# Batch 0's k, v and first expert products in plain f32, and a list scheduler for steps 0 to 17, in a fused attention and mixture-of-experts kernel

## The chip, the cores and the metric

The kernel runs on one core of a Trainium2 chip. Five engines matter here: TensorE (PE in the profile; its weight loads are the row PEld), VectorE (DVE), ScalarE (ACT), GpSimd (POOL), and SyncE (SP), which issues all DMAs of this kernel. Each engine takes its instructions in the order in which the program lists them; engines wait for each other by semaphores.

The metric is the time of one execution in microseconds on the device, as a median of several runs. The profiled execution is one further run, with a time of its own. Its span goes from the first instruction to the last, and the time is a little longer than the span.

## The reference

An attention through 32 memory slots per head, and behind it a mixture of four experts on its output:

```python
# q, k, v: (8, 8, 576, 64)   phi: (8, 8, 576, 32)
a = softmax(phi, axis=2)                                # over the sequence
k_m = einsum('bhsm,bhsd->bhmd', a, k)
v_m = einsum('bhsm,bhsd->bhmd', a, v)
attn = softmax(scale * (q @ k_m.T), axis=-1)            # over the 32 slots
x = (attn @ v_m), heads side by side -> (4608, 512)
p = domain_probs / (domain_probs.sum(-1) + 1e-9)        # (4608, 4)
for e in range(4):                                      # w1: (4, 512, 1024), w2: (4, 1024, 512)
    h = maximum(x @ w1[e], 0)
    out += p[:, e:e+1] * (h @ w2[e])
```

Everything is f32 at the boundary of the kernel.

## The kernel before, in words

**Tiling.** Batches go in four pairs. For each pair and each expert there are 32 steps: two batches, two halves of the rows (256 and 320 rows, or the other way round), eight blocks of 128 of the expert's 1024 hidden columns. That makes 512 steps (LAST). A step s has two parts on TensorE. `first(s)` (L485) makes a block of the hidden layer: six products of 256 or 320 columns. `second(s)` (L489) multiplies it by w2: six products of 512 columns, or nine where an odd batch also closes the tile that the two batches share. `first` runs two steps ahead of `second` (AHEAD), so step s issues `first(s + 2)` and then `second(s)`. Since x = attn · v_m, the kernel never forms x: it multiplies v_m by w1 beforehand (the tile vw), and `first` multiplies the transposed attention (the tile AT) by vw.

**Splits.** Products run in the rounded type fp32r. To keep f32 precision, each operand is split in two: ScalarE copies it rounded (the "hi" part), VectorE or GpSimd subtracts that from the operand (the "lo" part), and a product is made of three: hi·hi, hi·lo, lo·hi (lines L403 to L405, L459 to L461 and L500 to L502). Transposes and scores (L342) are plain f32.

**The beginning.** Before step 0, batch 0 needs: phi's softmax, its transposes (`phi_turn`, L212, and `phi_turn_tail`, L226, into the tile a), splits of k and v (`kv_split`, L249, and `tail_split`, L236), their products with a (`kv_mm`, L259), the folding of the partial sums by transposes (`kv_out`, `kv_fold`, `kv_pick`, L276 to L303) into the tile kvT, scores and softmax (`scores_mm`, L334, `scores_exp`, `soft`), the transposed attention AT (`transposes`, L380), and for one half of the hidden columns (fh = 0) the splits of w1 and the product of v_m with w1 (`vw_mm`, L400, evicted by `vw_out` and `vw_out_by_copy`, L423 and L428). This part is listed by hand from L1292 on. Between its pieces stand matmuls that only keep TensorE busy (`keep_warm`, L1284): 10, 4, 6 and 4 of them.

**Steps 0 to 17** (MANUAL is 18). Beside their own work they carry the remaining work of batch 0 (two more score tiles, the second half of w1 and vw, three quarters of w2) and the whole chain of batch 1, which is needed from step 14 on. REST_0 and UNITS_1 say in which step each whole unit is emitted; within a step the units come first, then `first(s + 2)`, then `second(s)` (L1369). The order on each engine is then made by the compiler's own scheduler. From step 18 on, `schedule()` (L602) has assigned every single operation to a step, and `run_step` (L1237) lists them in a fixed order.

**Loads.** All weights and inputs come through rings of staging buffers (`ring`, L84; `stage_ahead`, L95). A load is issued on SP's queue as soon as the buffer it goes to is free. The first nine loads (`early`) are k and v of batch 0 in four parts, their last 64 rows (kvt), q, two parts of w1 and one of w2. Batch 1 needs the split w1 again: before, the split tiles of the start are kept in SBUF and also written to DRAM (`keep_w1`, L146) for later pairs.

## Time and profile before

| | |
|---|---|
| median of 3 runs | 1372.82 us (1372.54 to 1373.73) |
| the profiled execution's own time | 1374.13 us |
| its span | 1372.4 us |
| granted TensorE clock, mean | 0.999 |
| stores and loads | HBM read 131.41 MB, written 26.21 MB |

The page of the profile gives busy times per engine over the whole span, a chain of work that ended last (followed back from the last instruction), and groups of instructions by line. TensorE's busy time is pipelined, so that consecutive matmuls overlap in the records: the interval between the starts of two matmuls is what one costs, not its duration. The windows view cuts the span into stretches, and the timeline lists the instructions in order with their start, their duration and, in brackets, the idle time of the engine before them and what ended it. Where a row is merged (x8), its duration is that of the whole run of instructions. A plain f32 product stands in the records as two matmuls, an f32 transpose as one.

### The profile page before, as it was taken

What the parts mean: (1) busy time and instruction counts of PE and PEld (TensorE: products, weight loads), DVE (VectorE), ACT (ScalarE), POOL (GpSimd) and SP (SyncE); (2) the same over time, 40 slices, a digit from 0 to 9 for tenths busy, and PEclk for the clock granted to TensorE, in tenths of its full rate; (3) what the DMA queues carried; (4) which work ended last, traced back from release to release, by engine and by line L of the source; (5) the groups of instructions that cost most, each with busy time, mean ns of one, the idle gap of its engine ahead of it and who ended that gap; (6) DMA issues with size and microseconds to landing.
All of it is one profiled execution on the core that took longest, in us unless ns stands there. A gap on an engine that the chain in (4) does not pass through costs nothing.

```text
span 1372.4 us, 21779 instructions
## 1 busy us (share of the span) xinstructions
PE 1356.9 (99%) x7444; PEld 1186.9 (86%) x7444; DVE 834.0 (61%) x1851; ACT 742.7 (54%) x1739; POOL 27.0 (2%) x27
## 2 busy tenths in 40 slices
PE   7999999999999999999999999999999999999998
PEld 6888888888888888888888888888888888888887
DVE  7667667577676656657567565665666644444532
ACT  7545555456556556655555656565655645455321
POOL 4300000000000000000000000000000000000000
PEclk9999999999999999999999999999999999999999
DMA  7627364344666466562664756555465635446101
GB/s 287 227 85 235 98 199 126 111 138 148 170 191 184 141 184 173 159 194 73 185 175 136 219 159 185 146 174 151 146 179 160 174 96 175 128 131 162 31 32 39
DMA packets 102398, 209.41 MB, mean 153 GB/s; under 512 B 18192, under 2 KB 18576, under 8 KB 102288
## 3 DMA queue, kind: packets, MB, share of 16 engines
q1 hardware_dynamic: 102288, 208.03, 50.6%
q8 instruction: 59, 0.97, 0.3%
q14 instruction: 51, 0.42, 0.1%
HBM read 131.41 MB, written 26.21 MB: 115 GB/s over the span
## 4 chain that ended last, share of the span: by engine, by line
PE 95%; DMA 2%; DVE 1%; ACT 1%; SPq 0%; issue 0%; ACTq 0%; DVEq 0%
PE p L501 19%; PE p L502 19%; PE p L500 19%; PE p L459 10%; PE p L461 10%; PE p L460 10%; PE pv L714 3%; PE x L267 2%; PE sT L1030 1%; DMA stage<-w 1%; PE sc L342 1%; PE pv L403 1%; PE pv L405 1%; PE pv L404 1%; DMA stage<-in_kv 0%
## 5 line engine op out<-in xcount | busy, mean ns | idle before, releaser
L481 DVE SCALAR_TENSOR_TENSOR h<-p,h 128x256 fp32r<-128x256 f32 x512 | 215.6, 421 | 319.8 <-ACT h L475 186.9
L501 PE MATMUL p<-w,h 128*128 128x512 f32 x1024 | 404.0, 395 | 0.0
L502 PE MATMUL p<-w,h 128*128 128x512 f32 x1024 | 401.9, 393 | 0.2 <-DVE nm L190 0.2
L500 PE MATMUL p<-w,h 128*128 128x512 f32 x1024 | 401.7, 392 | 0.0
L475 ACT ACTIVATE h<-p 128x256 fp32r<-128x256 f32 x512 | 196.3, 384 | 322.3 <-PE p L461 299.4
L459 PE MATMUL p<-AT,vw 128*128 128x256 f32 (+1 forms) x1024 | 305.7, 299 | 3.0 <-DVE h L481 1.6
L460 PE MATMUL p<-AT,vw 128*128 128x256 f32 (+1 forms) x1024 | 302.2, 295 | 0.6 <-DVE AT L395 0.6
L461 PE MATMUL p<-AT,vw 128*128 128x256 f32 (+1 forms) x1024 | 301.5, 295 | 0.1
L502 PEld LDWEIGHTS p<-w,h 128*128 128x128 f32 x1024 | 192.2, 188 | 43.3 <-DVE nm L190 0.5
L459 PEld LDWEIGHTS p<-AT,vw 128*128 128x128 f32 x1024 | 192.4, 188 | 24.5 <-issue 3.0
L500 PEld LDWEIGHTS p<-w,h 128*128 128x128 f32 x1024 | 192.4, 188 | 23.0
L501 PEld LDWEIGHTS p<-w,h 128*128 128x128 f32 x1024 | 192.6, 188 | 22.7 <-DVE w L155 0.2
L460 PEld LDWEIGHTS p<-AT,vw 128*128 128x128 f32 x1024 | 193.5, 189 | 17.7 <-DVE AT L395 0.8
L461 PEld LDWEIGHTS p<-AT,vw 128*128 128x128 f32 x1024 | 192.6, 188 | 0.3 <-issue 0.3
L722 ACT COPY E<-pv 128x512 f32<-128x512 f32 x192 | 111.4, 592 | 76.8 <-PE pv L714 46.2
L481 DVE SCALAR_TENSOR_TENSOR hm<-p,hm 128x64 fp32r<-128x64 f32 x256 | 56.1, 219 | 155.8 <-ACT h L475 155.7
L475 ACT ACTIVATE hm<-p 128x64 fp32r<-128x64 f32 x256 | 56.9, 222 | 110.8 <-PE p L461 110.6
L710 ACT CAST w<-stage 128x1024 fp32r<-128x1024 f32 x96 | 100.7, 1049 | 4.2 <-DMA stage<-w 4.2
L796 DVE TENSOR_TENSOR w<-stage,w 128x512 fp32r<-128x512 f32 x120 | 79.4, 683 | 0.0
L792 ACT CAST w<-stage 128x512 fp32r<-128x512 f32 x120 | 73.3, 616 | 5.2 <-DMA stage<-in_w 4.9
L776 DVE TENSOR_TENSOR vw<-rows,vw 128x512 fp32r<-128x512 f32 x96 | 64.6, 685 | 10.7 <-ACT vw L772 10.0
L517 DVE SCALAR_TENSOR_TENSOR acc<-p,pt,acc 128x512 f32<-128x512 f32 x96 | 67.3, 742 | 2.7 <-PE p L502 2.6
(135 smaller groups left out, 1321.8 us busy)
## 6 DMA issues: line engine op xcount, KB each, us to landing
stage<-w SPq DMA_DIRECT2D x96, 512.0 KB, 4.2
rows<-E SPq DMA_DIRECT2D x768, 64.0 KB, 2.7
stage<-in_w SPq DMA_DIRECT2D x80, 512.0 KB, 4.4
stage<-in_kv SPq DMA_DIRECT2D x32, 512.0 KB, 4.5
w<-w SPq DMA_DIRECT2D x64, 256.0 KB, 4.7
out<-acc SPq DMA_DIRECT2D x32, 256.0 KB, 4.1
stage<-in_qh SPq DMA_DIRECT2D x24, 288.0 KB, 3.2
ph<-in_phi SPq DMA_DIRECT2D x16, 288.0 KB, 4.1
```

Source lines behind the costliest of these rows:

```text
L459: nc.tensor.matmul(ps, w[:, 0, f], at_t[:, g, 0, c], start=g == 0, stop=False)
L460: nc.tensor.matmul(ps, w[:, 0, f], at_t[:, g, 1, c], start=False, stop=False)
L461: nc.tensor.matmul(ps, w[:, 1, f], at_t[:, g, 0, c], start=False, stop=g == 1)
L475: nc.scalar.activation(t[:, 0, to], ps[:, at_], AF.Relu)
L481: nc.vector.scalar_tensor_tensor(t[:, 1, to], ps[:, at_], 0.0, t[:, 0, to].bitcast(F32), ALU.max, ALU.subtract)
L500: nc.tensor.matmul(po[t], x[:, 0, :], w[:, 0, :], start=j == 0, stop=False)
L501: nc.tensor.matmul(po[t], x[:, 0, :], w[:, 1, :], start=False, stop=False)
L502: nc.tensor.matmul(po[t], x[:, 1, :], w[:, 0, :], start=False, stop=j == NJ - 1)
L710: nc.scalar.copy(w, raws[key])
L722: nc.scalar.copy(box["E"][:, i, :], box[i])
L792: nc.scalar.copy(t[:, 0, :], raws[key][:, i, :])
L796: nc.vector.tensor_sub(t[:, 1, :], raws[key][:, i, :], t[:, 0, :].bitcast(F32))
```

## The change

Three things change, all of them in the beginning and in steps 0 to about 21.

1. **Batch 0's products of a with k and v, and of v_m with the first expert's w1, are made in plain f32** from the staged data. There are no splits of k, v, kvt and w1 for these, and no folding: `direct_mm` puts k (or v) on the stationary side and gets the transposed result at once, which `direct_pick` copies into kvT. `direct_vw` makes vw from two plain f32 products of 512 columns, with both heads of a tile in one product, and evicts it in whole tiles. kvt of batch 0 is loaded in 64 rows instead of 128.
2. **Steps 0 to 17 are ordered by a list scheduler of single operations**, `start_plan`: each copy, subtraction, product, eviction and load is a task with an engine, a duration, predecessors and buffers; a simulated clock picks per engine the task that can start, the most urgent first. The resulting order is the order in the program. Tasks that don't fit before step 18 are emitted in steps 18 to 21. The warm-up matmuls after the first ten are gone.
3. **Who does what, and when it is loaded, changes with it.** Since the first w1 is no longer split, w1 of expert 0 is loaded a second time for batch 1 and split then (four `lo` parts on VectorE, four on GpSimd). Seven of the eight `lo` parts of the first w2 go to GpSimd; those of batch 1's k, v and kvt go from GpSimd to VectorE. The probabilities are loaded before k, and batch 1's phi before w1.

The core of the diff:

```diff
+SPLIT_KV = ("DVE",) * 8
+SPLIT_W2 = ("DVE",) + ("POOL",) * 7
+SPLIT_W1 = ("DVE", "POOL") * NP
...
+LOADS = [("w1", 0, 1, 0), ("w1", 0, 1, 1), ("qm", 0, 1), ("w2", 0, 1), ("w2", 0, 2), ("qt", 0), ("w2", 0, 3)]
+LOADS += [("kvt", 1), ("kv", 1, 0), ("kv", 1, 1), ("kv", 1, 2), ("w1", 0, 0, 0, 1), ("kv", 1, 3)]
+LOADS += [("qm", 1, 0), ("w1", 0, 0, 1, 1), ("qm", 1, 1), ("w1", 0, 1, 0, 1), ("w1", 0, 1, 1, 1), ("qt", 1)]
...
+    def direct_turn_out(g):
+        nc.scalar.copy(st["af"][:, 2 * g:2 * g + 2, :4], st["tpa", 0, g].rearrange("p c a m -> p a c m"))
...
+    def direct_mm(hp, w, raw, tail):
...
+        x, af = st["xd", w, hp // 2][:, hp % 2, :], st["af"]
+        for c in range(4):
+            nc.tensor.matmul(x, raw[:, c, w, :], af[:, hp, c], start=c == 0, stop=False)
+        nc.tensor.matmul(x, tail[:64, hp, w * P:w * P + P], af[:64, hp, 4], start=False, stop=True)
...
+    def direct_vw(fh, g, raw, tag):
+        ps = psum.tile([P, 512], F32, name="pv", tag=tag[0], bufs=tag[1])
+        for i in range(2):
+            nc.tensor.matmul(
+                ps, st["vf"][:, g, P * i:P * i + P], raw[:, i, :], start=i == 0, stop=i == 1
+            )
+        return ps
+
+    def direct_vw_hi(ps, fh, g):
+        vw[0, 0, fh, g] = att.tile([P, 2, 512], F32R, name="vw", tag="vw0", bufs=4)
+        nc.scalar.copy(vw[0, 0, fh, g][:, 0, :], ps)
+
+    def direct_vw_lo(ps, fh, g):
+        t = vw[0, 0, fh, g]
+        nc.vector.tensor_sub(t[:, 1, :], ps, t[:, 0, :].bitcast(F32))
+
+    def direct_pick(g, w, i):
+        kvd, x = kvT[0][:, w, 2 * g:2 * g + 2], st["xd", w, g]
+        r, m = slice(64 * i, 64 * i + 64), slice(M * i, M * i + M)
+        (nc.vector.tensor_copy if i and w == 0 else nc.scalar.copy)(kvd[r, :, m], x[r, :, m])
...
+        while left:
+            best = None
+            for eng in free:
+                cand = None
+                for t in left:
+                    if t.eng != eng or any(d.end is None for d in t.deps):
+                        continue
+                    at0 = max([free[eng]] + [d.end + (0 if d.eng == eng else 200 if d.eng == "PE" else 130) for d in t.deps])
...
+                    if t.sb and eng in lock:
+                        at0 = max(at0, lock["POOL" if eng == "DVE" else "DVE"] - 150)
+                    k = (max(at0, free[eng] + START_LOOK) if at0 > free[eng] + START_LOOK else free[eng], due[t])
+                    if cand is None or k < cand[0]:
+                        cand = k, at0, t
+                if cand and (best is None or cand[1] < best[1]):
+                    best = cand
...
     load_phi(0)
+    nc.sync.dma_start(pt, prob)
     with tc.manual_schedule():
...
-        for s in range(AHEAD):
-            first(s)
-        probabilities()
-    load_phi(1)
-    for s in range(MANUAL):
-        run_plan(s)
-        first(s + AHEAD)
-        second(s)
-    released.update(range(count[1]))
-    stage_released()
+        for t in first_tasks:
+            run_task(t)
```

## The prediction

> **What bounds the kernel now.** I read the page first: the busy shares and the chain that ended last.

> ```profile
> span 1372.4 us, 21779 instructions
> PE 1356.9 (99%) x7444; PEld 1186.9 (86%) x7444; DVE 834.0 (61%) x1851; ACT 742.7 (54%) x1739; POOL 27.0 (2%) x27
> PE 95%; DMA 2%; DVE 1%; ACT 1%; SPq 0%; issue 0%; ACTq 0%; DVEq 0%
> ```

> TensorE is busy 99% of the span and makes 95% of the chain. The change does nothing after step 21 but place a few operations anew, so what it can win is time in which TensorE does less than it could before the end of step 17. I looked for that in the chain of the first 60 us, which also shows what precedes the first hidden block:

> ```profile
> 1.65 6.21 DMA stage<-in_kv
> 7.88 1.15 ACT kvs L255 x2
> 9.05 1.35 DVE kvs L256
> 10.92 0.68 DVE a L224
> ...
> 13.23 1.71 PE x L267 x8
> ...
> 18.16 1.08 PE sc L342 x8
> ...
> 19.72 0.27 ACT kvT L297
> ...
> 20.99 1.12 PE sc L342 x8
> ...
> 25.50 1.27 issue
> ...
> 28.80 0.70 DVE AT L395
> 29.54 0.38 PE p L460
> ...
> 58.79 0.94 PE x L267 x8
> ```

> The first product with k starts near 11 us, although k landed at 7.86 (1.65 + 6.21): splits by ScalarE and VectorE stand between. The scores are complete at 22.1, and `first(0)` goes on only when AT's lo part is written at 29.5. Where step 0 begins and step 17 ends, the timeline of TensorE says:

> ```profile
> 31.25 0.28 PE L459 MATMUL p<-AT,vw 128*128 128x256 f32 x1
> ...
> 35.51 0.28 PE L459 MATMUL p<-AT,vw 128*128 128x256 f32 x1
> ...
> 36.22 0.40 PE L500 MATMUL p<-w,h 128*128 128x512 f32 x1
> ```

> ```profile
> 94.99 0.31 PE L459 MATMUL p<-AT,vw 128*128 128x320 f32 x1
> ...
> 95.87 0.39 PE L500 MATMUL p<-w,h 128*128 128x512 f32 x1
> ...
> 97.26 0.39 PE L500 MATMUL p<-w,hm 128*128 128x512 f32 x1
> ...
> 97.94 0.32 PE L459 MATMUL p<-AT,vw 128*128 128x320 f32 x1
> ```

> 31.25 is the first matmul of `first(2)`, which opens step 0; at 97.94 step 17's `second` has ended. Between lie 66.7 us. A narrow `first` costs 0.71 us (35.51 to 36.22), a wide one 0.88, six products with w2 1.39, nine 2.07. Side work comes from the groups of TensorE from 31.25 to 97.5 us:

> ```profile
> L342 PE MATMUL sc<-kvT,stage 128*128 128x64 f32 (+1 forms) x64 | 7.0, 260 | 0.0
> L403 PE MATMUL pv<-w,vt 128*128 128x512 f32 x12 | 5.2, 432 | 0.0
> L267 PE MATMUL x<-kvs,a 128*128 128x256 f32 x32 | 4.6, 283 | 0.0
> L388 PE MATMUL tp<-ident,at 128*128 128x128 f32 (+1 forms) x14 | 2.1, 268 | 0.0
> L218 PE MATMUL tpa<-ident,ph 128*128 128x128 f32 x8 | 1.4, 275 | 0.6 <-DVE ph L203 0.6
> ```

> By start-to-start intervals the steps' own work is 6 x 0.71 + 12 x 0.88 + 16 x 1.39 + 2 x 2.07 = 41.2 us. The side work is 64 score records at 0.11 (1.73 us for 16 in the row below), 36 vw products (three lines of 12) at 0.23, 32 kv products at 0.118 (58.79: 0.94 for eight), and some 36 short ones (14 + 8 shown, 14 more) at 0.11: 7.0 + 8.3 + 3.8 + 4.0 = 23.1. So 64.3 of 66.7 us are work and **2.4 us are lost** inside the steps. The larger loss lies before 31.25.

> ```profile
> 37.08 0.23 PE p L500
> ...
> 37.77 1.73 PE sc L342 x16
> ```

> **The change, part by part.** Loads and clock come first, from the windows view (columns: length, then busy us and instruction count of PE, PEld, DVE, ACT, POOL, then the granted TensorE clock, DMA share, GB/s).

> ```profile
> 10.00:15.00 5.00, 3.71 (x19) 3.45 (x20) 4.60 (x7) 4.46 (x10) 4.58 (x3) 0.69 1.03 418
> 15.00:20.00 5.00, 4.71 (x40) 4.54 (x40) 3.08 (x8) 2.64 (x10) 1.28 (x2) 0.97 1.03 401
> ...
> 8.50:11.91 3.41, 0.85 (x7) 0.85 (x8) 2.85 (x4) 3.41 (x9) 2.84 (x3) 1.00 1.03 419
> 11.91:15.33 3.42, 3.19 (x15) 2.92 (x15) 3.02 (x4) 2.69 (x6) 3.03 (x2) 0.50 1.03 414
> ...
> 31.25:40.00 8.75, 8.75 (x59) 7.54 (x58) 8.72 (x23) 5.19 (x12) 0.00 (x0) 1.00 0.57 193
> 40.00:50.00 10.00, 8.89 (x48) 7.18 (x47) 8.59 (x21) 7.46 (x16) 5.11 (x4) 1.00 0.79 270
> ...
> 60.00:70.00 10.00, 10.00 (x64) 8.66 (x63) 2.94 (x11) 4.97 (x17) 5.08 (x4) 1.00 0.71 204
> 70.00:97.50 27.50, 27.50 (x162) 23.99 (x161) 19.85 (x48) 11.53 (x30) 0.00 (x0) 1.00 0.29 92
> ```

> *Loads.* DMA moves 401 to 418 GB/s, so 512 KB take 1.28 us. The 72 KB of probabilities now go ahead of k (+0.2), kvt is halved (-0.6), batch 1's phi (576 KB) goes ahead of w1 (+1.4). Landings after that: k/v part 0 at 8.1, kvt 8.7, parts 1 to 3 at 10.0, 11.2, 12.5, q 13.8, phi 15.2, w1 16.5 and 17.7, w2 19.0. SP now waits for the phi transposes (8.4 us) before it issues phi and w1; the queue still holds 5 us of data then, so this costs nothing; without that cover w1 would be late by the wait.

> *Phi.* The transposes end at 8.34 (7.96 + 0.38 below). Three ScalarE copies without subtractions follow (0.58, 0.58, 0.37), on an engine that no longer splits k meanwhile: the last ends at 9.1, and the first direct product starts at 9.3 instead of 11.

> ```profile
> 7.96 0.38 PE L230 MATMUL tpb<-ident,ph 128*128 128x128 f32 x2
> ...
> 8.93 0.58 ACT L223 CAST a<-tpa 128x512 fp32r<-128x512 f32 x1
> ```

> *Direct k and v.* 40 plain f32 products of 64 columns, the form of the scores: two records of 0.108, 0.216 each, 8.7 us. Before it was 36 products in fp32r at 0.118 (4.2 us) and eight folds: more TensorE work, but without a hand to ScalarE and VectorE. It keeps up with the loads: k of part 3 can be multiplied by 13.7, the picks take two copies of 0.27 (the row at 19.72), and scores (1.7 us) end by 15.7 instead of 22.1. From there AT took 7.4 us (22.1 to 29.5), with other subtractions between its links on VectorE; even so it would be there by 23.1. v fills TensorE meanwhile.

> *Direct vw.* Two products per tile, 512 columns in plain f32, which no row shows. Lower bound: two records at the fp32r price, 0.46 for a product. Upper: eight times the 64-column product, 1.73. But a record of 64 columns costs as much (0.108) as a transpose of 128 (0.11), so the time doesn't grow with the columns from 64 on; two records of four times 0.11 are 0.88. I take 0.92, next to that row, and keep 1.73 as an end that this speaks against. Two tiles before `first(0)`: 3.7 us; two later ones: 3.7, in place of 12 fp32r products of 0.23 (2.8), so **+0.9** among the side work. For all eight products the ends are worth -3.7 and +6.5 us, half of it before step 0.

> [...]

> *The start as a sum.* TensorE is nearly dense from 9.3: 8.7 + 1.7 + 3.7 + 0.45 (transposes) = 14.6, to 23.9. Then hi (0.58), lo (0.69) and three hand-overs of 0.2: `first(0)` at 25.8. In that gap a side product of second-half vw (1.84 us, its w1 landing near 21) fits. `first(0)` and `first(1)` take 1.4: **step 0 at 27.2 instead of 31.25**.

> *Steps 0 to 17.* Work 41.2 + 23.1 + 0.9 - 1.8 (already done) = 63.4. VectorE, 8.72 of 8.75 us busy from 31.25 to 40, loses the first w1's lo parts and seven of w2's eight, and takes ten of batch 1's; ahead of step 0 it loses all splits. GpSimd gets eleven subtractions (SPLIT_W2, SPLIT_W1). I take a loss of 3.0 us: 2.4 as now and 0.6 because the order is fixed on assumed durations. Any task moved to steps 18 to 21 is the same work later, and TensorE has no idle cover to lose there; I count it at zero. The second load of w1 (2 MB, 5 us of DMA) and its eight splits fall where DMA runs at 92 to 204 GB/s, and its splits replace those of the first; should they be late, they delay vw of batch 1, and with it step 14.

> The sum: 27.2 + 63.4 + 3.0 = 93.6 against 97.94: **-4.3 us**. Profiled execution: 1374.13 - 4.3 = 1369.8. That execution lies 1.3 above the median, so against 1372.82 the forecast is **1368.5**.

> *The clock.* From 11.91 to 15.33 the granted clock was 0.50, after a window of equal length (8.50 to 11.91) in which TensorE was busy for 0.85 us only. The change takes 14 warm-ups away after that point, but begins at 9.3: about 2.6 of 3.4 us busy in that window. I count full clock. [...]

> **The rivals.**
> - *The new order holds without waits* (1366): loss in steps 1 us or less, second-half work fills the gaps of the start. 27.2 - 0.3 + 63.4 + 1.0 = 91.3, -6.6. For it: VectorE is relieved where it was full. Against: nothing shows that the list's durations hold.
> - *The clock is halved once* (1370.2): TensorE idles too long before 9.3, or the two-record products count for less. One window of 3.41 us at half speed costs 1.7. Against: 2.6 us of work in the window.
> - *The start's gain is given back* (1371.5): every side product stands in a fixed place directly behind its producer. Some 45 such pieces; if each second one comes 0.15 us late, 3 us more are lost (45 / 2 x 0.15 = 3.4). For it: the 0.6 us of idle before L218 in the groups above are exactly such a wait.
> - *VectorE sets the pace: slower* (1377). From 31.25 on to 50 it is 17.3 of 18.75 us busy already, and the list adds ten subtractions of 0.70 for batch 1 (7.0 us) and four of w1 (2.8). If the hidden block's lo part queues behind them, four PSUM buffers fill up and TensorE stops. It decides when more than 7 us of that isn't covered; the seven lo parts of w2 and four of w1 that go in these steps (7.7 us) speak against it.

> That the splits weren't on the path is excluded by the chain (7.88 to 11.6). That loads end later than the products is possible only for w1 (17.7), which leaves 5 us.

> **How the numbers follow.** Forecast 1368.5: 0.50. No waits 1366: 0.15. Clock 1370.2: 0.05. Given back 1371.5: 0.20. Slower 1377: 0.10. A measurement tells apart about 0.2%, 2.7 us: faster means under 1370.1. Faster: 0.50 + 0.15 + about half the clock case = 0.68; same 0.22; slower 0.10. The range goes from 1364.5 (no waits, and f32 products at the lower end before step 0, -1.8) to 1373.0 (given back, and half of the dearer end before step 0, +1.6).

> **What would show it.** Right: first direct product near 9.3; scores done by 16; step 0's first matmul at 26.5 to 28; a direct 512-column product of about 0.92; step 17's end at 92.5 to 94.5; clock 1.00 from 8.5 on. Wrong: TensorE idle in front of side products, for more than 4 us in sum; `first(0)` after 29; VectorE at 100% with TensorE waiting for L481's successor; or a time after step 21 that differs from before by over 1 us.

## The result, and the profile after

The change makes the kernel slower. Six runs gave 1382.01 us (1380.01 to 1382.88) beside 1373.52 us (1372.54 to 1376.94) for six runs of the kernel before; the ratio is 1.0055, with a 95% interval of 1.0042 to 1.0068. The forecast was 1368.5 us. The profiled execution took 1380.01 us with a span of 1378.2 us, 5.8 us longer than before.

The page of the changed kernel, span, busy times and the chain that ended last:

```profile
span 1378.2 us, 21742 instructions
PE 1368.0 (99%) x7444; PEld 1193.0 (87%) x7444; DVE 826.4 (60%) x1834; ACT 733.4 (53%) x1723; POOL 16.3 (1%) x20
...
PE 96%; DMA 2%; DVE 1%; ACT 1%; issue 0%; SPq 0%; ACTq 0%; DVEq 0%
```

The engines that the change relieves are relieved (VectorE 834.0 to 826.4 us, ScalarE 742.7 to 733.4), and TensorE is busy for 11.1 us longer, in the same number of matmul records. So some matmuls take longer, or longer ones stand where shorter ones stood. The chain of the first 60 us shows which:

```profile
3.21 7.88 DMA stage<-in_kv
11.13 1.10 PE xd L278 x8
12.24 0.36 PE xd L279 x2
...
14.25 1.90 PE xd L278 x8
16.15 0.62 PE xd L279 x2
16.76 1.90 PE sc L408 x8
...
30.23 5.55 PE pv L292 x8
35.78 0.44 PE tp L457 x4
```

From 11 us to beyond 50 us the chain is TensorE alone: the splits are gone from it, as forecast. But the same eight records of a direct product of k (L278) take 1.10 us at 11.13 and 1.90 us at 14.25. The granted clock gives the reason, in the windows view cut at the borders where the clock changes (columns as in the prediction: length, busy us and records of PE, ..., granted clock, DMA share, GB/s; the records are all that reach into the window, so those cut by its borders are counted too):

```profile
10.18:13.59 3.41, 2.69 (x21) 2.35 (x20) 0.23 (x1) 0.20 (x1) 0.00 (x0) 1.00 1.02 404
13.59:17.00 3.41, 3.41 (x15) 3.06 (x14) 0.00 (x0) 0.20 (x1) 0.00 (x0) 0.50 1.04 406
...
23.83:27.24 3.41, 3.41 (x15) 3.06 (x15) 1.63 (x5) 1.89 (x6) 0.00 (x0) 0.50 0.38 127
...
30.66:34.07 3.41, 3.41 (x5) 1.35 (x4) 0.00 (x0) 0.82 (x5) 0.00 (x0) 0.50 0.74 269
34.07:37.48 3.41, 3.41 (x13) 1.67 (x12) 1.74 (x3) 1.57 (x3) 0.00 (x0) 1.00 0.94 300
```

The clock halves at 13.59 and stays at 0.50 until 34.07, for 20.48 us. Before, the one stretch at half clock was 3.42 us long (11.91 to 15.33); 20.48 is six times 3.41, and I call that length a window. In all six TensorE is busy 100% of the time. Six windows at half speed are 10.2 us of TensorE's time, and that is about what step 0 is late (its first matmul, and that of `first(20)`, which opens step 18, in the timeline of TensorE):

```profile
40.51 0.68 PE L518 MATMUL p<-AT,vw 128*128 128x256 f32 x1
...
105.96 0.41 PE L518 MATMUL p<-AT,vw 128*128 128x320 f32 x1
```

Step 0 begins at 40.51 instead of 31.25, 9.3 us later, and 13.3 us later than the forecast 27.2. Steps 0 to 17 take 65.5 us instead of 66.7, so that step 18 opens 8.0 us later; 5.8 of these are left at the end of the span, since the two executions also differ by some 2 us behind step 18. The medians lie 8.5 apart.

### The profile page after: what moved, and what is told of

Its sections match the earlier page's. It is cut to its first block, busy times and chain, and to the rows that moved or that the text cites. A ratio compares the mean times of both kernels' runs of the same rounds, so it can differ in the third digit from the quotient of the medians.

```text
span 1378.2 us, 21742 instructions
## 1 busy us (share of the span) xinstructions
PE 1368.0 (99%) x7444; PEld 1193.0 (87%) x7444; DVE 826.4 (60%) x1834; ACT 733.4 (53%) x1723; POOL 16.3 (1%) x20
## 4 chain that ended last, share of the span: by engine, by line
PE 96%; DMA 2%; DVE 1%; ACT 1%; issue 0%; SPq 0%; ACTq 0%; DVEq 0%
PE p L564 19%; PE p L562 19%; PE p L563 19%; PE p L518 10%; PE p L520 10%; PE p L519 10%; PE pv L1174 3%; PE x L339 2%; PE sT L1490 1%; PE xd L278 1%; PE pv L292 1%; DMA stage<-in_kv 1%; DMA stage<-w 1%; PE sc L408 0%; PE pv L481 0%; PE pv L483 0%
```

## The experiments

The theories first. **A**: the clock follows the columns that are streamed through the array in a window, so that products of 64 columns, each record of which comes with a weight load of its own (PE x7444 and PEld x7444 on the page), count for little. **B**: the clock fell because TensorE was idle now and then for a load (2.69 of 3.41 us busy from 10.18 to 13.59), whatever the form of the products. The expectations also name **C**: plain f32 counts for little in any form.

**Loops of one form (e1_forms).** The kernel before, with loops ahead of it whose result is not read:

```diff
+        for _ in range(16):
+            full(512)          # plain f32, 512 moving columns
+        for _ in range(64):
+            full(64)
+        for _ in range(64):
+            full(128)
...
+        for _ in range(120):
+            rounded(256)       # fp32r
```

> The kernel before, with TensorE loops ahead of everything, dense and waiting for nothing: 16 plain f32 products of 512 columns, 64 of 64 columns, 64 of 128 columns, 64 of 64 columns, 120 fp32r products of 256 columns, then 13 times (five plain f32 of 64, one fp32r of 512) and 13 times (five of 64, three of 512). Some 100 to 150 us longer, so only the granted clock by window counts. Theory A (the clock follows the columns that stream through the array in a window, not the time for which TensorE is busy): 1.00 in the 512 block, 0.50 in both 64 blocks from their second window on, 1.00 in the 128 block and the fp32r block, 1.00 in the last. Theory B (the clock fell because of the idle gaps at 10.4 and before 13.6, the form of the products doesn't matter): 1.00 throughout after the first window. Theory C (plain f32 counts for little in any form): 0.50 in the blocks of 512, 64 and 128 columns, 1.00 from the fp32r block on.

Measured: the clock was 1.00 through all blocks, the dense 64-column ones too. That is what B had forecast. It speaks against A as I had put it, and against C and every other reading by which the plain f32 form lowers the clock by itself. A window of the first 64 block:

```profile
25.16:28.57 3.41, 3.41 (x33) 3.41 (x32) 0.00 (x0) 0.00 (x0) 0.00 (x0) 1.00 0.00 0
```

Counted from the timeline by what lies inside the window, with records at its borders by their share, these are some 1960 columns; all counts of columns below are made so. In the changed kernel, the first five windows at half clock hold 840 to 980, because there each record takes 0.2 us and more instead of 0.11. So I changed A to **A2**: one border on the columns per window, at whatever clock. A dense run of 64-column products lies just above it at full clock, and below it at half clock, where it can't get out again.

**Twice the columns (e2_wide).** The direct products of k and v multiply by the matrices a of both head pairs of a tile, and half of the result is not read:

```diff
-            nc.tensor.matmul(x, raw[:, c, w, :], af[:, hp, c], start=c == 0, stop=False)
+            nc.tensor.matmul(x, raw[:, c, w, :], af[:, two, c], start=c == 0, stop=False)
```

> The changed kernel, with 128 moving columns in each direct product of k and v in place of 64 (the matrices a of both head pairs of a tile; half of the result is not read). Same number of products, loads and waits. A: the record of 128 columns costs as much as one of 64 (0.11 us at full clock), the clock stays at 1.00, step 0 begins at 27 to 29 us in place of 40.5, the time falls by 9 to 13 us against the changed kernel, to about 1370 (3 us under the kernel before). B: the clock still halves at about 13.6, comes back one window later; 1374. C: nothing changes, 1380 to 1383.

Measured: 1373.34 us (1371.69 to 1374.75) beside 1374.29 for the kernel before, ratio 0.9987 (0.9978 to 0.9996); 8.7 us under the changed kernel, whose six runs were made in another session. In the profiled execution step 0 begins at 33.7, and the clock fell once and came back after one window. That is the course and the time that B had forecast; A had the clock held and 1370:

```profile
8.33:11.74 3.41, 2.13 (x15) 1.62 (x14) 0.77 (x3) 0.85 (x2) 0.00 (x0) 1.00 1.03 320
11.74:15.16 3.42, 3.42 (x16) 2.97 (x15) 0.23 (x1) 0.21 (x1) 0.00 (x0) 0.50 1.02 399
15.16:18.57 3.41, 3.41 (x26) 2.93 (x25) 0.75 (x2) 0.21 (x1) 0.00 (x0) 1.00 1.03 407
```

At half clock, 16 records of 128 columns bring the clock back, where 15 to 17 records of 64 did not for four windows in a row, at the same busy time. With busy time and records alike, the columns of a record are what differs, so idle time (B) is not what keeps the clock down. For the first fall this run can't tell the two theories apart: the window had 2.13 us busy, and with that only some 1650 columns.

**Filler products (e3_fill1, e4_fill3).** One, or three, bf16 products of 512 columns behind each group of five direct products, their result not read:

```diff
         nc.tensor.matmul(x, tail[:64, hp, w * P:w * P + P], af[:64, hp, 4], start=False, stop=True)
+        for _ in range(1):
+            nc.tensor.matmul(st["fill"], fill, fill.unsqueeze(1).broadcast_to([P, 4, P]), start=True, stop=True)
```

> The changed kernel, with one bf16 product of 512 columns (0.22 us) behind each group of five direct products, eight in all, their result not read. Columns per window rise from about 950 to 2000. A: the clock is held at least from some window on, if the border lies under that; the span is 1369 to 1376. B and C: 0.50 up to about 34 us as before, span 1380.

> The same with three such products behind each group (24 in all, 5.2 us of TensorE time at full clock). A: columns per window of about 3500; clock 1.00 throughout, step 0 begins near 32, span 1373 to 1375. B: halved once at 13.6. C: held as well, because bf16 counts.

Measured, one run each: 1372.2 us (span 1370.4) and 1375.81 us (span 1374.0), the clock at 1.00 throughout in both, as A had it; step 0 at 31.1 and 34.1 (near 32 was expected of the second). Since the fillers also stand in the waits, these two say little against B.

**The border by itself (e5_forms2).** Loops again, now with 32 columns in between:

```diff
+        for _ in range(16):
+            full(512)
+        for _ in range(96):
+            full(32)
+        for _ in range(64):
+            full(64)
+        for _ in range(32):
+            full(128)
+        for _ in range(64):
+            full(64)
```

> The kernel before, with dense TensorE loops ahead of everything: 16 plain f32 products of 512 columns, 96 of 32, 64 of 64, 32 of 128, 64 of 64 columns, none with a gap. Theory A2 (one border on the columns streamed in a window of 3.41 us, at whatever clock; the windows so far put it between 1200 and 1900 recorded columns, and a dense run of 64-column products has 1950 at full clock but 970 at half): 1.00 in the 512 block; the clock halves one window after the 32 block begins (about 960 columns at full clock, TensorE 100% busy); stays 0.50 through the 32 block and the first 64 block; back to 1.00 one to two windows into the 128 block; stays 1.00 in the last 64 block. Theory B (only idle gaps lower the clock): 1.00 throughout.

Measured, in windows of the 512 block, the 32 block (two), the first 64 block, its end with the 128 block, the 128 block, and the last 64 block:

```profile
9.25:12.67 3.42, 3.42 (x9) 1.51 (x9) 1.35 (x1) 0.24 (x1) 1.07 (x1) 1.00 1.03 420
19.49:22.91 3.42, 3.42 (x33) 3.42 (x33) 0.00 (x0) 0.00 (x0) 0.00 (x0) 1.00 0.00 0
22.91:26.32 3.41, 3.41 (x18) 3.41 (x18) 0.00 (x0) 0.00 (x0) 0.00 (x0) 0.50 0.02 5
63.87:67.28 3.41, 3.41 (x18) 3.41 (x18) 0.00 (x0) 0.00 (x0) 0.00 (x0) 0.50 0.00 0
80.93:84.34 3.41, 3.41 (x18) 3.41 (x18) 0.00 (x0) 0.00 (x0) 0.00 (x0) 0.50 0.00 0
84.34:87.76 3.42, 3.42 (x32) 3.42 (x32) 0.00 (x0) 0.00 (x0) 0.00 (x0) 1.00 0.00 0
91.17:94.59 3.42, 3.42 (x33) 3.42 (x32) 0.00 (x0) 0.00 (x0) 0.00 (x0) 1.00 0.00 0
```

All five points of A2 came true. After a window of 33 records of 32 columns, without a gap, the clock halves (22.91). It stays there through the 32 block and the whole first 64 block (63.87: some 1020 columns). It returns with the 128 block (84.34). The last 64 block, which differs from the first only in that it begins at full clock, keeps it (91.17: some 1960 columns). The same products hold two different clocks, 0.50 at 63.87 and 1.00 at 91.17, by the clock at which they begin. B is refuted: TensorE is 100% busy in all seven windows.

The kernel behind the loops shows the same of a window with waits. In e1 and in e5 the first products with k of the kernel before (fp32r, 256 columns) fall differently into the windows; each pair of lines is one such window and the next:

```profile
120.73:124.14 3.41, 1.70 (x13) 1.28 (x12) 2.48 (x4) 3.41 (x8) 2.31 (x2) 1.00 0.50 173
124.14:127.55 3.41, 3.41 (x18) 3.41 (x18) 3.16 (x4) 2.36 (x6) 2.04 (x2) 0.50 0.49 161
```

```profile
108.24:111.65 3.41, 1.91 (x14) 1.73 (x14) 2.53 (x5) 3.41 (x8) 2.75 (x2) 1.00 0.54 173
111.65:115.06 3.41, 2.49 (x22) 2.29 (x21) 3.41 (x4) 1.80 (x5) 1.61 (x1) 1.00 0.55 201
```

1.91 us busy keep the clock in e5, where 2.69 us lost it in the changed kernel. So the first fall can't be put down to idle time either. Columns fit, if a column of fp32r counts about half of one in a plain f32 record: some 2400 of them lost the clock in e1 and some 3400 kept it in e5, beside some 1210 plain f32 columns that lost it in the changed kernel. That half is an estimate from these windows alone. In time, too, a plain f32 record of 512 columns is twice one of fp32r (0.44 against 0.23 us).

**Fillers in the waits alone (e6_gapfill), and with the width (e7_widefill).** Two fillers behind the first k group and one behind the second; once with products of 64 columns, once (e7) on top of the edit of e2, with 128.

```diff
+        for _ in range({(0, 0): 2, (1, 0): 1}.get((hp, w), 0)):
+            nc.tensor.matmul(st["fill"], fill, fill.unsqueeze(1).broadcast_to([P, 4, P]), start=True, stop=True)
```

> The changed kernel with two bf16 products of 512 columns behind the first group of direct products and one behind the second, which lie in the wait for the loads of k, their result not read. A2: columns of the window that fell rise from 1216 to about 2500, the clock mostly stays at 1.00 (the windows' place differs from run to run), step 0 begins at 29 to 31 us in place of 40.5, the step part is unchanged, the time is 2 to 4 us under the kernel before. B: the same for the first fall. If the 64-column groups can't hold the clock even so: 0.50 from 17 to 34 us, time 5 us over the kernel before.

> The same three products, and 128 moving columns in the direct products of k and v. A2: columns well above the border in every window, clock 1.00 in nearly every run; step 0 at 29 to 30.5, time 2.5 to 4.5 us under the kernel before and less spread than without. B: as without the width.

Measured without the width: 1378.22 us, from 1372.05 to 1384.21, in twelve runs, beside 1375.04 (ratio 1.0022, 1.0003 to 1.0041). That is a miss: 2 to 4 us under the kernel before were expected. This spread goes with the clock. The six fastest runs (1372.05 to 1377.47) had a mean granted clock of 0.995 to 0.999, the four slowest (1381.11 to 1384.21) 0.991 to 0.992. One window of half clock in 1380 us is 0.0012 of the mean, so 0.991 is some seven windows. In the profiled execution the fall comes later, in a window without any gap:

```profile
14.72:18.13 3.41, 3.41 (x29) 3.28 (x29) 1.96 (x6) 1.92 (x5) 0.00 (x0) 1.00 1.04 411
18.13:21.54 3.41, 3.41 (x28) 3.14 (x27) 2.58 (x6) 2.06 (x6) 0.00 (x0) 1.00 0.88 288
21.54:24.96 3.42, 3.42 (x8) 1.79 (x7) 2.27 (x2) 1.42 (x6) 1.32 (x1) 0.50 0.85 301
```

Both windows are 100% busy with 64-column records. By what lies inside, some 1770 columns kept the clock and some 1620 lost it. With e2, where some 1650 lost the clock (8.33) and some 1730 at half clock brought it back (11.74), and with a window of e9 that held with some 1680,

```profile
13.78:17.19 3.41, 3.41 (x29) 3.21 (x27) 1.79 (x4) 0.85 (x2) 0.00 (x0) 1.00 1.05 410
17.19:20.60 3.41, 3.41 (x29) 3.19 (x27) 1.53 (x3) 1.89 (x6) 0.00 (x0) 1.00 0.97 309
```

With the width: **1372.60 us (1371.71 to 1373.54), ratio 0.9984 (0.9975 to 0.9993)**, the fastest version of those with more than one run. The clock was 0.999 or 1.000 in all eleven runs, as A2 has it; the fillers are those of e6, so the width is what differs. The gain of 2.4 us is just under what was expected (2.5 to 4.5): step 0 begins at 31.2 and not at 29 to 30.5.

**The half clock of the kernel before (e8_beforewarm).** Ten more warm-up matmuls behind the phi transposes of the kernel before:

```diff
+        keep_warm(10)
```

> The kernel before with ten more warm-up matmuls behind its phi transposes, where TensorE waits from 8.3 to 10.9 us. A2 and B: its one window at half clock (11.9 to 15.3) is gone; what that window cost: at most 1.7 us, and less because splits and loads end last there; 0 to 1.5 us under the kernel before. If it gains nothing, the half clock in the kernel before cost nothing.

Measured: 1374.90 beside 1375.04 us, ratio 1.0001 (0.9992 to 1.0009). The clock was 1.00 in the profile, step 0 began at 30.2 instead of 31.25, and step 18 opened at 98.04, no earlier than before (97.94). So the one halved window cost the kernel before nothing. The kernel before does scatter by its clock, though: over 67 runs beside these experiments it was 0.996 to 1.000, with medians of 1378.5 at 0.996, 1375.5 at 0.997 and 1374.1 to 1374.6 from 0.998 up. Where the further halved windows of those runs lay isn't known.

**Spread fillers, and eight fillers in more runs (e9_spread, e10_fill1b).** Five fillers behind four of the eight groups, the width left at 64 columns; and the kernel of e3 once more, in twelve runs.

```diff
+        for _ in range({(0, 0): 2, (2, 0): 1, (0, 1): 1, (2, 1): 1}.get((hp, w), 0)):
+            nc.tensor.matmul(st["fill"], fill, fill.unsqueeze(1).broadcast_to([P, 4, P]), start=True, stop=True)
```

> The changed kernel with 64 columns again and five bf16 products of 512 columns, their result not read: two in the wait behind the first k group, one each behind the third k group and the first and third v group. A2 (border between 1660 and 1730 recorded columns a window, a dense 64-column window being hardly above it): every window from 8 to 22 us gets at least 500 more; clock 0.998 to 1.000 in at least 9 of 10 runs, where the three products before left it between 0.991 and 0.999. Groups cost 1.29 us against 1.46 with 128 columns: step 0 at 30 to 30.7, 0.5 to 1 us ahead of the wide one, time 2.5 to 4 us under the kernel before. If some runs still fall, they lie 1.7 us up for each halved window.

> The kernel with one such product behind each of the eight groups again, timed in rounds. A2: the clock is held in all runs (2100 or more columns in every window in its profile), step 0 at 31.1, time 1.5 to 3 us under the kernel before: the gain that is left of the change when the clock is held and 1.5 us of fillers are paid. If the change's gain at full clock were the 4.3 us of the forecast, it would come 3 us under or more even with the fillers.

Measured: 1372.79 us (1371.08 to 1383.76) and 1378.72 us (1372.35 to 1386.30) beside 1374.48; ratios 0.9994 (0.9979 to 1.0009) and 1.0035 (1.0012 to 1.0059). In e9 ten of eleven runs were at 0.998 to 1.000 as expected, one at 0.991 and 1383.76 us; the time (1.7 us under, and an interval that reaches over 1) and step 0 (31.0) fell short of what was expected. e10 is a miss: six of twelve runs had 0.990 or 0.991 (1382.76 to 1386.30). The other six held the clock at 0.998 to 1.000 and took 1372.35 to 1374.68. A2 has a reading for it, which no trace shows: at half clock groups take nearly twice as long (2.51 us from 14.18 to 16.69 in the changed kernel, 1.40 from 11.13 to 12.53), so a filler in each adds too little to come back, and one fall in any early window is enough. Which window that was isn't shown, since the profiled execution of e10 was one that held.

Eight or five fillers alone therefore don't make it safe; the width with three of them held in all eleven runs. Between the middle of the held and that of the fallen runs of e10 lie some 12 us (1372.9 against 1384.7), for a mean clock lower by 0.009, or seven windows: 1.7 us a window, as half of 3.41 would have it.

## Why the prediction was wrong

**The step that failed** is the one on the clock: "The change takes 14 warm-ups away after that point, but begins at 9.3: about 2.6 of 3.4 us busy in that window. I count full clock." The busy time was right (2.69 of 3.41), but busy time isn't what went with the clock: windows that were 100% busy lost it too (e5 at 19.49, e6 at 18.13). The window held some 1210 columns, and by my estimate 1650 to 1700 were needed. The row I had (0.85 us busy, then 0.50) fits busy time and columns alike, and I didn't ask which. The direct products were priced as the scores, by records of 0.108 us; the same row shows that 64 columns cost as much as 128 (0.108 and 0.11), and so that half of the columns are streamed per time. A wait in that window came on top: k of part 1 landed at 11.1 (3.21 + 7.88 in the chain above) and not at 10.0, and TensorE stood idle for 0.72 us before it. e6 lost the clock without any wait, so the wait alone isn't the cause.

One rival named the event: "*The clock is halved once* (1370.2): TensorE idles too long before 9.3, or the two-record products count for less. One window of 3.41 us at half speed costs 1.7." It had the event, but not the mechanism: the fall followed the window from 10.18 and not idling before 9.3, and two-record products of 512 columns held the clock at 1.00 (e1), so it is the width of 64 columns that counted for little. Its size was off too: not one window but six (and some seven in the fallen runs of e10), because the products didn't raise the clock again from half (0.50 from 13.59 to 34.07). 0.05 was too small a chance, for a form of product that the kernel before never ran for a whole window. The slower rival, VectorE as the bound, didn't happen. Two stretches of the changed kernel's steps, the first ones and those in which VectorE is busiest (same columns):

```profile
40.51:50.00 9.49, 9.49 (x65) 8.31 (x64) 5.77 (x17) 5.48 (x12) 5.11 (x5) 1.00 0.45 146
...
80.00:90.00 10.00, 9.02 (x51) 7.40 (x51) 8.89 (x20) 6.42 (x14) 3.25 (x3) 1.00 0.85 274
```

VectorE is busy for 5.77 of 9.49 and 8.89 of 10 us. TensorE stands idle for 0.98 us in the second, nearly all of it in one wait for VectorE's part of a hidden block:

```profile
PE tp L457 <- DVE hm L540: 0.9, 1, 0.9
```

**The rest of the sum** can be read from e9, whose profiled execution held the clock. Its start, step 0 and step 18 in the timeline of TensorE:

```profile
8.38 1.08 PE L279 MATMUL xd<-af,stage 128*128 128x64 f32 x8
...
12.05 1.10 PE L279 MATMUL xd<-af,stage 128*128 128x64 f32 x8
13.08 0.43 PE L280 MATMUL xd<-af,stage 64*128 64x64 f32 x2
13.45 0.39 PE L282 MATMUL fill<-fill 128*128 128x512 bf16 x1
...
22.59 3.70 PE L295 MATMUL pv<-stage,af 128*128 128x512 f32 x8
26.13 0.60 PE L460 MATMUL tp<-ident,at 128*128 128x128 f32 x4
...
27.88 0.68 PE L521 MATMUL p<-AT,vw 128*128 128x256 f32 x1
...
29.70 1.88 PE L295 MATMUL pv<-stage,af 128*128 128x512 f32 x4
31.02 0.68 PE L521 MATMUL p<-AT,vw 128*128 128x256 f32 x1
```

```profile
96.40 0.41 PE L521 MATMUL p<-AT,vw 128*128 128x320 f32 x1
```

- *First direct product at 9.3*: 8.4 here, 8.92 in the changed kernel. Right, a little early.
- *A group of five products, 1.08 us*: from 12.05 to the filler at 13.45 are 1.40 us. The four products over 128 rows take 1.03 of these, for 0.86 assumed; the one over the last 64 rows takes 0.37, not 0.216. In the single records the excess lies where the rows change: 0.20 us from the last record over 128 rows to the first over 64, and as much back, where two records over 128 rows are 0.11 apart. By the starts, and without the wait in the first, the eight groups take 1.29 to 1.40 us each, 10.9 in place of 8.7: mis-sized by 2.2.
- *A product of 512 columns in plain f32, 0.92 us*: four in 3.54 us (22.59 to 26.13), 0.89. Right, and with it the choice between the bounds. The 0.92 was an estimate next to 0.88, and no row of before shows it. Its premise, that the time doesn't grow with the columns from 64 on, holds only up to 128: a record of 128 columns takes 0.108 us (four transposes from 26.13 to 26.56), one of 512 takes 0.44.
- *Step 0 at 27.2, with one side product of vw ahead of it*: 31.02, with both of them ahead (1.8) and 0.7 of fillers outside the waits. Without these 28.5, or 1.3 over the forecast: 2.2 for the groups and 0.9 for the wait for the first loads, with the two fillers in it (9.46 to 9.81 and 10.15 to 10.65), less 0.9 for the early start and some 0.8 in the products of vw and between the transposes and `first(0)` (26.13 to 27.88). The three hand-overs of 0.2 in the forecast's sum are shown by no run: in the changed kernel the records of AT's transposes end at 36.22 and the first product with AT's lo part starts at 37.90, which leaves some 0.4 us beside hi (0.59) and lo (0.68).
- *Work in the steps*: both side products lie before step 0, so 61.6 us of work instead of 63.4, in 65.4 us. The loss is 3.8 us instead of 3.0 (2.4 before). That is somewhat more than assumed for the list's fixed order; the wait for the hidden block shown above, 0.8 us in this run, is a part of it, and the rest wasn't broken down.
- *Step 18*: 96.40 instead of the forecast 93.6, and 1.5 us under the kernel before. The 1.3 of the start, 0.7 of fillers and 0.8 of loss make the 2.8.

In the changed kernel itself, 10.2 of the 13.3 us by which step 0 missed the forecast are the clock and 1.8 the second side product; the other 1.3 agree with e9.

So with the clock held, by fillers and width that cost time themselves, the change is worth some 2 us and not 4.3: 2.4 for e7 and 2.1 for the ten held runs of e9 against all runs of the kernel before, 1.8 and 1.9 against those of its runs that held 0.998 or more. How much of that is the plain f32 products and how much the list scheduler was not separated: no kernel had one without the other.

## What to carry to other kernels

Before a stretch of work is moved to TensorE, count the columns that its products stream in a clock window, not the time for which it is busy: here, by my estimate, 1650 to 1700 columns of plain f32 in 3.41 us were needed (about twice as many in fp32r, by few windows), and 64-column products streamed some 1960 at full clock and some 1020 at half (e5). Such a form held the clock but didn't bring it back: in the changed kernel, 20.48 us at half clock followed the window with the wait of 0.72 us for a load. The times of one program scattered too (1372 to 1386 us in e10). If products are about as long with twice the columns (the four over 128 rows took 1.09 us with 128 columns in e7, 8.28 to 9.37, and 1.03 with 64 in e9), use the columns, even if half of the result is thrown away, and read the granted clock next to the busy time in every window.

## What the runs showed of the hardware that I had not expected

- The granted clock had two values under the same dense work: 64-column plain f32 products ran at 1.00 (some 1960 columns a window) or at 0.50 (some 1020) until the block ended, by the clock at which they began (e5).
- The clock halved at 22.91 in e5, behind one window of nothing but products of 32 columns (33 records from 19.49), though TensorE was 100% busy, while fp32r products with waits between them, 1.91 of 3.41 us busy from 108.24, kept it at 1.00.
- A plain f32 product of 64 columns over 64 rows among products over 128 rows took 0.36 us, beside 0.22 to 0.26; the excess lies where the rows change, 0.20 us from record to record instead of 0.11 on either side (e9). Why wasn't looked into.
- The same program on the same chip took from 1372 to 1386 us (e10), with mean clocks from 1.000 to 0.990; what differed between its runs no trace shows.
